# Chunk attention and a bilinear feed-forward: float32 loads by 256-token unit on one hardware queue, casts on chip, eight units transposed by TensorE in a hand-written order, one attention slot per unit

## The chip, the cores and the metric

The kernel runs on one core of one Trainium2 chip. The metric is device time in microseconds (us) of one execution, the median of several. A profile comes from one execution; its span, first to last instruction, is about 2 us shorter than the time. Words used below: TensorE multiplies matrices (PE in the profile; PEld is its weight load), VectorE is DVE, ScalarE is ACT, GpSimd is POOL, and SP is the engine that issues the hardware DMA queue. PSUM is the memory that TensorE writes its results to; to evict is to copy them out of it.

## The reference, cut to what matters

```python
# q, k, v: (8, 8, 576, 64) float32; chunks of 64 tokens
scores = scale * q_c @ k_c.T           # per batch, head and chunk
attn = softmax(scores)
x = (attn @ v_c) as (4608 tokens, 512) # heads side by side
out = ((x @ w_a) * (x @ w_b)) @ w_out  # 512 -> 1536 -> 512
```

The kernel works on blocks of 512 tokens, nine in all. A block has two units of 256 tokens for the attention. The feed-forward part of a block is 12 column steps (8 matmuls each, two products and their multiplication) and 4 output steps (12 matmuls each). That makes 144 matmuls of 128x512 per block, 1296 in the program.

## The kernel before

Everything is loaded as float32 and cast to bf16 by the DMA itself, which is issued by GpSimd (the software queue). Units 0 to 3 are transposed by TensorE and later ones by a DMA transpose. TensorE's instructions are kept in the program's order:

```python
DMA_TRANSPOSE_FROM = 2                       # blocks 2 and up
...
nc.gpsimd.dma_start(out=dst[:, g0 + g],      # bf16 <- float32, 256-byte rows
    in_=src[bt, :, s0 + 128 * g:s0 + 128 * g + 128, :].rearrange("h p d -> p h d"))
...
if K >= DMA_TRANSPOSE_FROM:
    by_dma()
    return [scores, sums, values]            # three separate steps
return [by_pe, scores, sums, values]
...
for g in range(NG):                          # load order: block 0,
    load_rows(0, 128 * g, 128 * g + 128)
for i in range(3):
    load_ab_weights(512 * i, 512 * i + 512)  # all of w_a and w_b,
load_block(1)                                # block 1, then w_out, block 2
...
att = start_attention(K + 1) if K + 1 < NBLK else []   # while block K is fed forward
...
for i, s in enumerate(att):                  # TensorE order: from step 1 of the block on
    at.setdefault(1 + i * (n - 2) // len(att), []).append(s)
```

The softmax here doesn't subtract the row's maximum and nothing guards it: scores larger than these inputs give would overflow.

## Time and profile before

| | before |
|---|---|
| time, median of the first 3 runs | 354.98 us (354.16 to 356.6) |
| span of the profiled run | 352.6 us |
| first feed-forward matmul | 24.46 us |
| second unit pair needed by TensorE, and there | 31, 38.4 us |
| first DMA transpose needed, and there | 66, 70.9 us |
| period of a block later on | 33.9 us |

From the page of the kernel before: span, busy times, the span in 40 equal slices (each digit is the busy share in tenths; PEclk is the granted TensorE clock), and the chain of work that ended last. The clock record begins only at 30.0 us, so the PEclk digits before that say nothing: the first four feed-forward matmuls, at 24.46 in the timeline below, take 1.87 us, where later eight take 1.73.

```profile
span 352.6 us, 6180 instructions
...
PE 319.6 (91%) x2584; PEld 145.2 (41%) x2584; DVE 125.2 (36%) x167; ACT 118.3 (34%) x163; POOL 107.3 (30%) x134
...
PE   0545799499999999999999999999999999999994
...
PEclk9998599989999999999999999999999999999999
...
PE 85%; DMA 8%; POOL 5%; issue 0%; SPq 0%; DVE 0%; POOLq 0%
```

The first ten slices, 88 us, are where TensorE is not full. After them only its own work counts.

The stretch table of the kernel before: stretch, its length, busy time of each engine, granted clock, DMA share (the time of all packets over that of 16 engines; packets overlap, so it can be above 1), and GB/s.

```profile
10.00:12.00 2.00, 0.68 (x35) 0.43 (x33) 1.23 (x1) 0.00 (x0) 2.00 (x3) 1.00 2.29 146
18.00:20.00 2.00, 0.64 (x32) 0.55 (x33) 0.53 (x1) 0.72 (x1) 0.78 (x2) 1.00 1.23 207
90.00:120.00 30.00, 30.00 (x234) 13.31 (x232) 11.95 (x16) 12.08 (x18) 16.10 (x21) 1.00 1.88 168
```

GB/s counts written bytes. The cast halves them, so 146 and 207 are about 290 and 410 GB/s read.

The timeline of the kernel before, TensorE only (start, length, instruction, in brackets the idle time before it and what ended it):

```profile
24.46 1.87 PE L224 MATMUL mm<-xT,wb_sb 128*128 128x512 bf16 x4 [3.04 <-DVE xT L195]
34.15 0.58 PE L129 MATMUL att<-identity,q_raw 128*128 128x128 bf16 x4 [3.35 <-DMA q_raw<-in_q_dram]
38.38 0.61 PE L129 MATMUL att<-identity,k_raw 128*128 128x128 bf16 x4 [1.56 <-DMA k_raw<-in_k_dram]
70.88 0.60 PE L153 MATMUL att<-qkt 64*64 64x64 bf16 x32 [5.22 <-DMA qkt<-k_raw]
```

Feed-forward starts at 24.46. TensorE then waits for q and k of unit 2, and again at 66 to 71 for the transposed k of unit 4.

The same kernel's chain of waits in order of time (start, length, what), the loads that ended the first wait, and one step that comes once per block:

```profile
15.82 16.56 DMA wb_sb<-in_moe_w_b_dram
...
34.40 3.93 DMA k_raw<-in_k_dram
...
61.37 9.46 DMA qkt<-k_raw
...
97.34 0.38 PE att L187 x32
...
131.24 0.38 PE att L187 x32
```

The last weights land at 15.82 + 16.56 = 32.4 us and the k that TensorE needs at 38.3. One period is 131.24 - 97.34 = 33.9 us.

### The profile page before, as it was taken

How to read it: one execution, taken by the hardware profiler on the slowest of the kernel's cores; microseconds unless marked ns; L12 is line 12 of the kernel's file. 1: busy time of each engine (PE TensorE's matmuls, PEld its weight loads, DVE VectorE, ACT ScalarE, POOL GpSimd, SP SyncE). 2: the span in 40 equal slices, each digit the busy share in tenths (PEclk: the TensorE clock that was granted, in tenths of full speed). 3: DMA queues.
4: the chain of work that ended last, by engine and by line, in shares of the span. 5: the costliest groups of instructions: out<-in, count | busy, mean ns of one | idle time of the engine just before them, and what ended most of it. 6: DMA issues, size and time to landing. Idle time of an engine off the chain costs nothing.

```text
span 352.6 us, 6180 instructions
## 1 busy us (share of the span) xinstructions
PE 319.6 (91%) x2584; PEld 145.2 (41%) x2584; DVE 125.2 (36%) x167; ACT 118.3 (34%) x163; POOL 107.3 (30%) x134
## 2 busy tenths in 40 slices
PE   0545799499999999999999999999999999999994
PEld 0422344144444444444444444444444444444441
DVE  0321255214353434244333434343435343433331
ACT  1331146132525143434333434333442434311210
POOL 8924949396345865931200000000000000000000
PEclk9998599989999999999999999999999999999999
DMA  9999999999999999995933324320211111111213
GB/s 77 166 207 158 145 176 154 147 158 160 159 183 173 175 174 172 170 182 120 72 79 70 81 18 92 73 60 3 60 32 30 30 33 30 32 30 31 61 30 89
DMA packets 152603, 36.05 MB, mean 102 GB/s; under 512 B 143360, under 2 KB 147968, under 8 KB 152576
## 3 DMA queue, kind: packets, MB, share of 16 engines
q0 software_dynamic: 117248, 18.88, 73.2%
q1 hardware_dynamic: 35328, 16.79, 25.5%
q8 instruction: 20, 0.33, 0.4%
q14 instruction: 7, 0.06, 0.0%
HBM read 37.75 MB, written 9.44 MB: 134 GB/s over the span
## 4 chain that ended last, share of the span: by engine, by line
PE 85%; DMA 8%; POOL 5%; issue 0%; SPq 0%; DVE 0%; POOLq 0%
PE mm L224 52%; PE mm L241 27%; DMA wb_sb<-in_moe_w_b_dram 5%; DMA qkt<-k_raw 3%; PE att L153 2%; PE att L187 2%; PE att L168 2%; POOL q_raw L101 2%; DMA k_raw<-in_k_dram 1%; POOL v_raw L101 1%; POOL k_raw L101 1%; POOL wa_sb L66 1%; PE att L129 0%; POOL wb_sb L66 0%; SPq L138 0%
## 5 line engine op out<-in xcount | busy, mean ns | idle before, releaser
L224 PE MATMUL mm<-xT,wb_sb 128*128 128x512 bf16 x432 | 114.2, 388 | 3.0 <-DVE xT L195 3.0
L234 DVE TENSOR_TENSOR ab_sb<-mm,b_sb 128x512 bf16<-128x512 f32 x108 | 74.7, 692 | 116.9 <-PE mm L224 116.9
L233 ACT CAST b_sb<-mm 128x512 bf16<-128x512 f32 x108 | 63.3, 586 | 157.5 <-PE mm L224 157.5
L224 PE MATMUL mm<-xT,wa_sb 128*128 128x512 bf16 x432 | 112.9, 384 | 0.0
L241 PE MATMUL mm<-wo_sb,ab_sb 128*128 128x512 bf16 x432 | 100.2, 383 | 0.0
L224 PEld LDWEIGHTS <-wa_sb 128*128 128x128 bf16 x432 | 42.8, 99 | 52.7 <-issue 3.0
L241 PEld LDWEIGHTS <-ab_sb 128*128 128x128 bf16 x432 | 41.5, 99 | 50.7 <-issue 3.5
L224 PEld LDWEIGHTS <-wb_sb 128*128 128x128 bf16 x432 | 40.0, 99 | 50.0 <-issue 7.0
L249 DVE COPY o_sb<-mm 128x512 f32<-128x512 f32 x36 | 24.9, 692 | 79.4 <-PE mm L241 77.1
L160 ACT ACTIVATE E<-att 128x1024 bf16<-128x1024 f32 x18 | 18.4, 1024 | 48.8 <-PE att L153 48.8
L101 POOL DMA_DIRECT2D v_raw<-in_v_dram x32 | 28.7, 910 | 16.4 <-PE att L187 12.4
L101 POOL DMA_DIRECT2D k_raw<-in_k_dram x32 | 28.5, 902 | 15.8 <-DMA q_raw<-in_q_dram 7.5
L101 POOL DMA_DIRECT2D q_raw<-in_q_dram x32 | 28.8, 915 | 9.5 <-DMA q_raw<-in_q_dram 2.8
L195 DVE TENSOR_TENSOR xT<-att,rs 128x1024 bf16<-128x1024 f32 x18 | 21.9, 1217 | 9.3 <-ACT rs L177 9.3
L176 ACT ACTIVATE ln<-att 128x1024 f32<-128x1024 f32 x18 | 18.4, 1024 | 11.6 <-PE att L168 11.6
L177 ACT ACTIVATE rs<-ln 128x1024 f32<-128x1024 f32 x18 | 19.0, 1058 | 0.3
L153 PE MATMUL att<-qkt 64*64 64x64 bf16 x576 | 8.8, 205 | 8.2 <-DMA qkt<-k_raw 5.2
L129 PE MATMUL att<-identity,q_raw 128*128 128x128 bf16 x32 | 4.0, 284 | 13.2 <-DMA q_raw<-in_q_dram 12.5
L153 PEld LDWEIGHTS <-qkt 64*64 64x64 bf16 x576 | 6.7, 117 | 16.0 <-issue 6.3
L134 DVE COPY qkt<-att 128x2048 bf16<-128x2048 bf16 x4 | 4.9, 1222 | 16.9 <-PE att L129 16.8
L168 PE MATMUL att<-E,ones 64*64 64x512 bf16 x72 | 7.8, 424 | 2.3 <-ACT E L160 2.3
L187 PEld LDWEIGHTS <-v_raw 64*64 64x64 bf16 x576 | 6.8, 114 | 7.2 <-issue 6.7
(19 smaller groups left out, 46.6 us busy)
## 6 DMA issues: line engine op xcount, KB each, us to landing
out_dram<-o_sb SPq DMA_DIRECT2D x72, 128.0 KB, 2.4
q_raw<-in_q_dram POOLq DMA_DIRECT2D x32, 128.0 KB, 8.9
k_raw<-in_k_dram POOLq DMA_DIRECT2D x32, 128.0 KB, 7.8
v_raw<-in_v_dram POOLq DMA_DIRECT2D x32, 128.0 KB, 8.3
wa_sb<-in_moe_w_a_dram POOLq DMA_DIRECT2D x3, 512.0 KB, 11.1
wb_sb<-in_moe_w_b_dram POOLq DMA_DIRECT2D x3, 512.0 KB, 12.8
wo_sb<-in_moe_w_out_dram POOLq DMA_DIRECT2D x2, 768.0 KB, 10.1
q_raw<-in_q_dram POOLq DMA_DIRECT2D x8, 64.0 KB, 10.9
```

The costliest lines, as they stand in the source:

```text
L101: nc.gpsimd.dma_start(out=dst[:, g0 + g], in_=src[bt, :, s0 + 128 * g:s0 + 128 * g + 128, :].rearrange("h p d -> p h d"),)
L153: nc.tensor.matmul(sc[cl * 64:cl * 64 + 64, j, m, gg, :], qkt[j * 64:j * 64 + 64, 1, gg, m, cl * 64:cl * 64 + 64], qkt[j * 64:j * 64 + 64, ...
L160: nc.scalar.activation(out=E, in_=sc, func=AF.Exp, scale=scale)
L168: nc.tensor.matmul(sm[j * 64:j * 64 + 64, cl, :], ones[cl * 64:cl * 64 + 64, :], E[cl * 64:cl * 64 + 64, j].rearrange("p m g s -> p (m g s)"),
L176: nc.scalar.activation(out=ln.rearrange("p c m n -> p c (m n)"), in_=sm, func=AF.Ln)
L177: nc.scalar.activation(out=rs, in_=ln, func=AF.Exp, scale=-1.0)
L195: nc.vector.tensor_tensor(out=dst, in0=av.rearrange("p c m g s -> p c m (g s)"), in1=rs, op=mybir.AluOpType.mult,)
L224: nc.tensor.matmul(t[:, sp * w:sp * w + w], wt[:, kt, cols], xT[:, kt, sp * w:sp * w + w], start=(kt == 0), stop=(kt == NKT - 1),)
L233: nc.scalar.copy(out=b_sb, in_=ps[0])
L234: nc.vector.tensor_tensor(out=ab_tiles[K][:, ft, :], in0=ps[1], in1=b_sb, op=mybir.AluOpType.mult)
L241: nc.tensor.matmul(o_ps, ab_tiles[K][:, ft, tg * 128:tg * 128 + 128], wo_sb[:, ft, :], start=(ft == 0), stop=(ft == NFT - 1),)
L249: nc.vector.tensor_copy(out=o_sb, in_=o_ps)
```

## The change

The intent: all loads go as float32 through one hardware queue in an explicit order, so that what is needed first comes first, and the casts move to VectorE (units 0 to 7 and the weights) and GpSimd (later units). Eight units are transposed by TensorE instead of four. The order of TensorE's work in blocks 0 and 1 is written out by hand: block 0 is fed forward with only unit 2's transposes in between, and block 1 is done in two halves of 256 tokens. Sums of the last unit, scores of the next and values of the last follow each other in one slot, and all of PSUM is one pool of eight banks. Cut to its core:

```diff
-DMA_TRANSPOSE_FROM = 2
+PE_UNITS = 8
...
-            nc.gpsimd.dma_start(
-                out=dst[:, :, c0:c1],
+            staged[n, i] = wst_pool.tile([128, NKT, WCOL], FP32, name="wst")
+            nc.sync.dma_start(
+                out=staged[n, i],
...
+            eng = nc.vector if U < PE_UNITS else nc.gpsimd
+            eng.tensor_copy(out=raw[n, U], in_=staged.pop((n, U)))
...
+    def slot(s=None, f=None):
+        if f is not None:
+            sums(f)
+        if s is not None:
+            scores(s)
+        if f is not None:
+            values(f)
...
-    with tc.manual_schedule(engines={mybir.EngineType.PE}):
+    with tc.manual_schedule(engines={mybir.EngineType.PE, mybir.EngineType.SP}):
+        load_qk(0)
+        load_qk(1)
+        load_v(0)
+        load_v(1)
+        for i in range(3):
+            load_ab(i)
...
+        for i in range(NWP):                  # block 0
...
+            if i + 3 < NWP:
+                load_ab(i + 3)
+            if i == 3:
+                load(2)
+                load(3)
+            ab_step(0, 2 * i)
+            if i == 5:
...
+                cast(2, "qk")
...
+                transpose_pe(2)
+            ab_step(0, 2 * i + 1)
+        slot(2)
+        cast(2, "v")
+        load_v(5)
+        slot(None, 2)
...
+        seq = [lambda ft=ft: ab_step(1, ft, 0, 256) for ft in range(NFT)]
+        seq += [lambda ft=ft: ab_step(1, ft, 256, 512) for ft in range(NFT)]
...
+                seq.insert(12, lambda: slot(2 * K + 4, 2 * K + 3))    # blocks 2 to 7
...
+                seq.insert(4, lambda: slot(2 * K + 3, 2 * K + 2))
```

## The prediction

> **What bounds the kernel now.** The chain of waits is 85% TensorE, 8% DMA. The stretch table shows TensorE full (30.0 of 30 us) from 90 us on, and the chain repeats a block every 33.9 us: 144 feed-forward matmuls at 0.216 us (31.1 us) plus two attention units at 1.4 us, each in three pieces. The sum closes: last matmul 347.8 = 35.3 (effective start: feed-forward begins at 24.5 but only 2 of 12 steps run before TensorE waits, 31 to 38.4, for unit 2's q and k, queued behind all first weights) + 280 (1296 x 0.216) + 1.8 (half-clock matmuls at 38.8 to 42.4) + 19.6 (14 units x 1.4) + 3.7 (units 2, 3) + 7.5 (5.2 us waiting at 66 to 71 for the first DMA transpose, then a cold clock). The tail is 4.8. So about 43 us of 353 are start and stalls. Meanwhile written bytes run at 205 GB/s (twice that read) for weights but about 150 (300 read) for 256-byte q, k, v rows.
>
> **What the change does.**
> - Order and queue: q, k of units 0, 1 first, in 512-byte runs, then v, then weights in small pieces. The same read bytes at 300 to 400 GB/s put k of unit 1 at about 9 us, the first weights at 16, all a/b weights at 29, unit 2 at 34, before TensorE wants it. The start is then bound by the attention chain, not loads. VectorE keeps order: it casts unit 1 before it evicts unit 0's transposes. Estimate: scores 0 at 11.4, scores 1 at 15, xT at 22.5; feed-forward starts at 22.6 and should not stop: -12.7.
> - Casts on chip: 42 on VectorE, 30 on GpSimd. The Trainium skill ("VectorE: DVE Perf Modes", the perf-mode tier table) gives an fp32 SBUF copy twice the base rate, so I estimate 0.65 us for 1024 columns. In block 1 VectorE is then about 35 of 40 us busy: +3 of local stalls.
> - Transposes by TensorE for 8 units, not 4: 16 took 0.89 us, +4.5, but no wait for a DMA transpose and its cold clock: -7.5.
> - New wait: after block 0, unit 2 runs alone (scores, exp, sums, ln, exp, multiply) with nothing to fill TensorE: +4.4, perhaps +1 cold clock. Half-width matmuls in block 1: +0.5. Start clock +0.7.
> - One slot per unit: the three pieces cost 0.48, 0.44, 0.48 us, about 0.1 each for re-entering; the skill ("TensorEngine Tiling (Array Packing)", Key Properties) says changing tiling mode drains TensorE. I estimate 1.1 instead of 1.4: -4.8 over 16 units, less 1.5 for bunched evictions (8 shared PSUM banks).
>
> Sum: about -9.4, giving 345.6; the schedule looks hand-fitted, so some of my stalls may be absent: **343 us**, 8 in 10 within **334 to 352**. Faster by over 2%: **0.73**; within 2%: **0.23**; slower: **0.04**.
>
> **What would show it.** First feed-forward matmul at 21 to 24 us, no wait over 2 us in block 0; about 5 us idle once near 45 to 50 us; no wait for DMA transposes; period 33.2 to 33.6 us from block 3 on; casts 0.6 to 0.7 us; loads of q, k, v spread to the end.
>
> **What would make it wrong.** Hardware-queue loads of 256-byte runs well under 250 GB/s, or in-order waits of that queue (stores, transposes and loads share it) starving a unit: +5 to +15. Casts at 1.1 us: VectorE binds block 1, +5 to +8. Bunched evictions stalling each slot: the period stays 33.9. Against that, an earlier start or a cheaper slot: to 334.

## The result

The changed kernel takes 340.49 us (median of 4 runs, 340.02 to 340.7), the kernel before 354.57 in the same rounds. The ratio is 0.959, with a 95% interval of 0.9551 to 0.963. Here and below, a ratio is the mean time of one kernel's runs over that of the other's of the same rounds, so it is not quite the ratio of the medians. Executions over 1.5% slower than the fastest of the same kernel are left out of the means.

The page of the changed kernel, the lines that answer to those before:

```profile
span 338.6 us, 6687 instructions
...
PE 313.0 (92%) x2709; PEld 160.6 (47%) x2744; DVE 158.9 (47%) x251; ACT 129.8 (38%) x227; POOL 31.9 (9%) x36
...
PE   2459959999999999999999999999999999999994
...
PEclk9999996999999999999999999999999999999999
...
PE 90%; ACT 3%; DMA 2%; DVE 1%; issue 1%; SPq 1%
```

TensorE is now full from the fourth slice on, except for one dip in the sixth, and no DMA of importance is left in the chain.

Its timeline, TensorE only, the two waits of 1 us or more from the first feed-forward matmul to the end, and between them the place where TensorE starts on unit 2, without a wait:

```profile
22.31 0.59 PE L280 MATMUL ps<-xT,wb_307 128*128 128x512 bf16 x1 [3.10 <-DVE xT L241]
...
42.84 0.61 PE L164 MATMUL ps<-identity,q_raw 128*128 128x128 bf16 x8
...
51.14 1.01 PE L280 MATMUL ps<-xT,wb_307 128*128 128x256 bf16 x4 [3.30 <-DVE xT L241]
```

Its chain of waits, first where only unit 2 runs, then half-width matmuls at full clock, then one slot and the next one at the same place a block later:

```profile
45.63 0.44 PE ps L194 x32
46.07 1.07 ACT E L202 x2
47.19 0.43 PE ps L209 x3
47.62 1.07 ACT ln L219 x2
48.71 1.06 ACT rs L222
49.84 0.57 issue
50.41 0.69 DVE xT L241
51.14 5.23 PE ps L280 x24
...
62.76 7.09 PE ps L280 x64
...
134.99 0.34 PE ps L209 x4
135.33 0.28 PE ps L194 x32
135.61 0.32 PE ps L232 x32
...
168.16 0.34 PE ps L209 x4
```

Feed-forward starts 2.15 us earlier and runs through block 0. Then 5.5 us pass from the scores of unit 2 to the first matmul of block 1. The clock record has half clock from 49.4 to 56.2, and the 24 half-width matmuls after the wait take 5.23 us. Later 64 of them take 7.09, so 24 would take 2.66: the clock costs 2.6 us. The period is 168.16 - 134.99 = 33.17 us.

Two numbers speak against the reading that the loads which TensorE stood waiting for now come earlier. The trace's landings have the last piece of w_a and w_b at 32.4 us in both kernels, and k of unit 2 at 37.7 us (before: 38.3). What differs is that TensorE doesn't ask for unit 2 until 42.8 us. Only the very first loads are earlier: k of unit 1 lands at 9.25 us (before: 15.0), which goes with the earlier start. So the experiments below ask which part of the change did it.

### The profile page after: what moved, and what is told of

Its sections match the earlier page's. It is cut to its first block, busy times and chain, and to the rows that moved or that the text cites. A ratio compares the mean times of both kernels' runs of the same rounds, so it can differ in the third digit from the quotient of the medians.

```text
span 338.6 us, 6687 instructions
## 1 busy us (share of the span) xinstructions
PE 313.0 (92%) x2709; PEld 160.6 (47%) x2744; DVE 158.9 (47%) x251; ACT 129.8 (38%) x227; POOL 31.9 (9%) x36
## 4 chain that ended last, share of the span: by engine, by line
PE 90%; ACT 3%; DMA 2%; DVE 1%; issue 1%; SPq 1%
PE ps L280 56%; PE ps L296 27%; PE ps L164 2%; DMA k_in<-in_k_dram 2%; PE ps L209 2%; PE ps L194 2%; PE ps L232 1%; ACT rs L222 1%; ACT ln L219 1%; ACT qkt L172 1%; SPq L128 1%; DVE xT L241 1%; ACT E L202 0%; DVE qkt L172 0%; DVE k_raw L152 0%
## 5 line engine op out<-in xcount | busy, mean ns | idle before, releaser
L288 ACT CAST b_sb<-ps 128x512 bf16<-128x512 f32 (+1 forms) x120 | 64.3, 546 | 145.3 <-PE ps L280 121.6
L289 DVE TENSOR_TENSOR ab_sb<-ps,b_sb 128x512 bf16<-128x512 f32 (+1 forms) x120 | 75.6, 637 | 82.9 <-PE ps L280 80.2
L296 PEld LDWEIGHTS <-ab_sb 128*128 128x128 bf16 x432 | 42.2, 98 | 49.9
L304 DVE COPY o_sb<-ps 128x512 f32<-128x512 f32 x36 | 24.9, 691 | 54.8 <-PE ps L296 54.8
L241 DVE TENSOR_TENSOR xT<-ps,rs 128x512 bf16<-128x512 f32 x36 | 23.2, 686 | 30.1 <-ACT rs L222 30.1
L219 ACT ACTIVATE ln<-ps 128x512 f32<-128x512 f32 x36 | 19.7, 602 | 24.5 <-PE ps L209 24.5
L280 PE MATMUL ps<-xT,wb_307 128*128 128x512 bf16 (+1 forms) x79 | 20.3, 381 | 6.6 <-DVE xT L241 6.4
L152 POOL CAST q_raw<-q_in 128x1024 bf16<-128x1024 f32 x10 | 10.4, 1040 | 145.3 <-DMA q_in<-in_q_dram 130.2
L296 PE MATMUL ps<-wo_964,ab_sb 128*128 128x512 bf16 x72 | 21.4, 379 | 0.3
L296 PE MATMUL ps<-wo_1007,ab_sb 128*128 128x512 bf16 x72 | 21.4, 379 | 0.1
L296 PE MATMUL ps<-wo_1022,ab_sb 128*128 128x512 bf16 x72 | 21.4, 379 | 0.0
L296 PE MATMUL ps<-wo_992,ab_sb 128*128 128x512 bf16 x71 | 21.2, 379 | 0.0
L202 ACT ACTIVATE E<-ps 128x512 bf16<-128x512 f32 x36 | 19.3, 586 | 3.5 <-PE ps L194 3.5
L280 PE MATMUL ps<-xT,wa_309 128*128 128x512 bf16 (+1 forms) x80 | 20.5, 383 | 0.0
L296 PE MATMUL ps<-wo_949,ab_sb 128*128 128x512 bf16 x66 | 20.1, 379 | 0.3
L296 PE MATMUL ps<-wo_934,ab_sb 128*128 128x512 bf16 x67 | 20.3, 379 | 0.0
L280 PE MATMUL ps<-xT,wb_358 128*128 128x512 bf16 (+1 forms) x74 | 19.0, 365 | 0.3
L280 PE MATMUL ps<-xT,wa_360 128*128 128x512 bf16 (+1 forms) x80 | 19.2, 365 | 0.0
L280 PE MATMUL ps<-xT,wa_429 128*128 128x512 bf16 (+1 forms) x80 | 18.8, 358 | 0.4
L280 PE MATMUL ps<-xT,wb_461 128*128 128x512 bf16 (+1 forms) x74 | 18.6, 357 | 0.4
L280 PE MATMUL ps<-xT,wb_393 128*128 128x512 bf16 (+1 forms) x80 | 18.8, 358 | 0.0
```

The costliest lines, as they stand in the source:

```text
L152: eng.tensor_copy(out=raw[n, U], in_=staged.pop((n, U)))
L202: nc.scalar.activation(out=E_of[U][:, j], in_=sc[j], func=AF.Exp, scale=scale)
L219: nc.scalar.activation(out=ln[:, cl].rearrange("p m n -> p (m n)"), in_=sm[cl], func=AF.Ln)
L241: nc.vector.tensor_tensor(out=x_tiles[K][:, :, c0:c0 + 128], in0=av[cl].rearrange("p m g s -> p m (g s)"), in1=rs[:, cl], op=MULT,)
L280: nc.tensor.matmul(ps[n], w_ab[n, i][:, kt, o:o + 128], xT[:, kt, c0:c1], start=(kt == 0), stop=(kt == NKT - 1),)
L288: nc.scalar.copy(out=b_sb[:, :c1 - c0], in_=ps["wb"])
```

## The experiments

Theory A: the gain comes from TensorE's order in the first blocks, from the units that TensorE transposes itself, and from the slots. Theory B: it comes from the loads, that is from the hardware queue and the order of loading. The names b... are edits of the kernel before, a... of the changed one.

### b1_order: only TensorE's order in block 0

```diff
+            if K == 0:
+                for j, i in zip((0, 1, 4, 2, 5, 3, 6, 7), (7, 8, 8, 9, 9, 10, 10, 11)):
+                    at.setdefault(i, []).append(att[j])
+                att = []
```

> The kernel before with TensorE's order of block 0 changed alone: unit 2 and 3's attention steps come after feed-forward step 7 instead of after step 1. Loads, queue, casts untouched. Theory A (the wait from 31 to 38.4 us is TensorE's fixed order asking for unit 2 too early, not the loads being late): the wait goes, feed-forward still starts at 24.5 us, at most 1.5 us of waiting is left before block 1, time 354.6 - 7 to - 9, so 345.5 to 348. Rival B (the gain of the change comes from load order and the hardware queue): nothing much changes, within 2 us of 354.6.

Measured: 354.37 us, ratio 0.9985 (0.9949 to 1.0021). The same, as B said, but not for B's reason. The timeline of b1_order, the two waits of over 2 us that follow its first feed-forward matmul:

```profile
53.32 1.02 PE L224 MATMUL mm<-xT,wb_sb 128*128 128x512 bf16 x3 [2.19 <-DVE xT L195]
...
72.68 0.64 PE L153 MATMUL att<-qkt 64*64 64x64 bf16 x32 [15.75 <-DMA qkt<-k_raw]
```

The waiting between 31 and 38 us is gone, exactly as A said, and the wait for the DMA transpose of unit 4 grew from 5.2 to 15.75 us. It ends near the same time as before (72.7, was 70.9). TensorE reached the second wait earlier and stood there longer.

### b2_pe_transposes: only eight units transposed by TensorE

```diff
-DMA_TRANSPOSE_FROM = 2
+DMA_TRANSPOSE_FROM = 4
```

> The kernel before with 8 units transposed by TensorE instead of 4, nothing else. Theory: the 5.2 us wait for the first DMA transpose at 66 to 71 us and the half clock after it (together 7.5) go, four units more at 0.9 us on TensorE (+3.6): 350.7, range 349 to 352. Rival (the DMA transposes only wait because loads are late, so the wait moves to the loads of units 4 and 5): the wait stays at about 4 us near 66 us and the time is 354 to 358.

Measured: 350.96 us, ratio 0.9896 (0.9857 to 0.9934), the expected 350.7. The wait near 66 us is gone; the one from 31 to 38 us is still there. Its start in the timeline of b2_pe_transposes:

```profile
34.86 0.59 PE L129 MATMUL att<-identity,q_raw 128*128 128x128 bf16 x4 [4.43 <-DMA q_raw<-in_q_dram]
```

### b3_both: both edits

> The kernel before with both earlier edits: block 0's TensorE order changed and 8 units transposed by TensorE. In the order-alone run the 7.4 us wait at 31 to 38 us only moved: the wait for the DMA transpose of unit 4 grew from 5.2 to 15.7 us and ended at the same 72 us. Theory (two waits in series on one stream of loads and transposes, so each edit alone leaves the other in charge): together they give much more than the sum of 0.4 and 3.8: unit 4's k lands near 62 us instead of its transpose at 72.6, a wait of 3 to 6 us is left in block 1, time 345 to 349. Rival (the two edits just add): 350 to 351.

Measured: 344.71 us, ratio 0.9729 (0.9704 to 0.9753). Alone the edits gave 0.4 us, which is within the noise, and 3.8 us (354.74 the median of before in their rounds, 354.69 here), together 10.0. The longest wait on a DMA after the start of the timeline of b3_both is this:

```profile
59.06 0.40 PE L129 MATMUL att<-identity,k_raw 128*128 128x128 bf16 x4 [1.29 <-DMA k_raw<-in_k_dram]
```

The theory had expected 3 to 6 us of waiting in block 1, and the time came out just under its range.

The two waits were thus in series, and while the second stood, the first was worth nothing. The kernel still uses the old software queue, the old load order and the old three-piece attention. Ten of the fourteen microseconds come without any of them.

### a1_split: the slot undone in blocks 2 to 7

```diff
-                seq.insert(12, lambda: slot(2 * K + 4, 2 * K + 3))
...
-                seq.insert(4, lambda: slot(2 * K + 3, 2 * K + 2))
+                for at, s, f in ((12, 2 * K + 4, 2 * K + 3), (4, 2 * K + 3, 2 * K + 2)):
+                    seq.insert(at + 2, lambda f=f: values(f))
+                    seq.insert(at + 1, lambda s=s: slot(s))
+                    seq.insert(at, lambda f=f: sums(f))
```

> The changed kernel with the slot undone in blocks 2 to 7: sums, scores and values separated by one feed-forward or output step each. Theory (each re-entry from the small tiles to the full array costs about 0.1 to 0.2 us, three instead of one per unit): period 33.17 goes to 33.8 to 33.9, time 340.5 + 4 (12 slots x 0.35), 343.5 to 345.5. Rival (the shorter period comes from the shared PSUM banks and the changed evictions): period stays at 33.2, time within 1 us of 340.5.

Measured: 344.88 us, ratio to the kernel before 0.9712 (0.9679 to 0.9744); the changed kernel has 340.49. Its chain of waits, one place a block apart:

```profile
135.96 0.41 PE ps L209 x4
136.37 1.83 PE ps L280 x8
138.20 0.38 PE ps L194 x32
...
169.86 0.41 PE ps L209 x4
```

The period is back at 33.90 us, and the 4.4 us are 12 slots at 0.37 us. The sums, scores and values take 0.41 + 0.38 + 0.38 = 1.17 us apart, and 0.34 + 0.28 + 0.32 = 0.94 in one slot. The rest of the 0.37 is in the matmuls after each piece: the 8 after the sums take 1.83 us here, and 8 undisturbed ones 1.73, and this 0.1 us is paid three times instead of once. The shared PSUM pool stayed, so it is not what shortened the period by itself.

### a4_software_queue: the changed kernel's loads back on the software queue

```diff
-            staged[n, i] = wst_pool.tile([128, NKT, WCOL], FP32, name="wst")
-            nc.sync.dma_start(
+            staged[n, i] = wpool.tile([128, NKT, WCOL], BF16, name=f"{n}{i}")
+            nc.gpsimd.dma_start(
...
-            eng = nc.vector if U < PE_UNITS else nc.gpsimd
-            eng.tensor_copy(out=raw[n, U], in_=staged.pop((n, U)))
+            raw[n, U] = staged.pop((n, U))
```

The same for q, k, v and w_out; the units that TensorE transposes take two DMAs per piece instead of one, with 256-byte rows. The input tiles get more buffers (6 or 8, not 3), and the cast tiles are gone.

> The changed kernel with its loads back on the GpSimd software queue that casts in the DMA; no staging, no casts on VectorE or GpSimd; order of loads and of TensorE as in the change. Theory A (TensorE's order and the slots make the gain, the hardware queue and the casts on chip don't): first feed-forward matmul at 20 to 23 us (VectorE no longer casts unit 1 before it evicts unit 0), time 337 to 342. Rival B (the hardware queue makes the gain): q and k of unit 1 come later, first feed-forward matmul at 24 us or later, waits for loads in block 1, time 344 to 350.

Measured: three fast runs at 340.56 to 341.51 us, ratio 0.9604 (0.9573 to 0.9635), where the changed kernel has 0.959. The profiled run was a slow one (586.92 us): its clock record stands at 0.16 from 285.5 us to the end, and is like the others before that. There the first feed-forward matmul is at 21.72 us, and TensorE waits for unit 2 alone, as in the changed kernel:

```profile
21.72 0.59 PE L272 MATMUL ps<-xT,wb 128*128 128x512 bf16 x1 [3.10 <-DVE xT L233]
...
50.66 1.01 PE L272 MATMUL ps<-xT,wb 128*128 128x256 bf16 x4 [3.30 <-DVE xT L233]
```

So the hardware queue, the 512-byte runs and the casts on chip make none of the gain within 1 us. a4 keeps the new order of loads, and no run put the old order back alone: what that order is worth, in the earlier start above all, is not measured. The Trainium skill ("DMA: Bandwidth & Descriptors", Issuing engines are not separate DMA queues) says that DMAs of all issuing engines end up on the same 16 DMA engines and interleave. The 340.6 to 341.5 here fit that, but they are no test of it, because few waits for loads are left to shorten.

### a2_early_unit2: unit 2 inside block 0

```diff
         for i in range(3):
             load_ab(i)
+        load(2)
...
             ab_step(0, 2 * i)
+            if i == 3:
+                cast(2, "qk")
+                transpose_pe(2)
+            if i == 4:
+                slot(2)
+                cast(2, "v")
             if i == 5:
...
+                slot(None, 2)
             ab_step(0, 2 * i + 1)
-        slot(2)
...
-        slot(None, 2)
```

> The changed kernel with unit 2 loaded right after the third weight piece (the queue stood waiting there for a staging buffer) and its attention run inside block 0 (transposes after step 6, scores after step 8, sums and values after step 10) instead of alone after it. Theory (the 5.5 us at 45.6 to 51.1 in which only unit 2 runs, and the half clock of 6.8 us it brings, are pure loss): 340.5 - 4.4 - 2.6, so 333 to 335.5. Rival (weights now come later and block 0 stalls for them, or the clock drops anyway later): 337 to 341.

Measured: 339.43 us (338.29 to 340.68), ratio 0.957 (0.9535 to 0.9605). The rival was nearer: only 1.1 us came of the expected 5 to 7.5, and with runs spread over 2.4 us and an interval that holds the changed kernel's 0.959, even that is not clear of the noise. Two new waits, in its timeline:

```profile
37.17 1.39 PE L280 MATMUL ps<-xT,wb 128*128 128x512 bf16 x3 [2.06 <-DVE wb L85]
...
52.99 0.61 PE L280 MATMUL ps<-xT,wb 128*128 128x256 bf16 x4 [1.48 <-DVE xT L241]
```

The first is a wait for the cast of a weight piece, and half clock follows it (37.3 to 40.7 us in the clock record). Whether the weights came late or VectorE did is settled by a6 below.

### a3_pool_cast1: unit 1 cast by GpSimd

```diff
-            eng = nc.vector if U < PE_UNITS else nc.gpsimd
+            eng = nc.vector if U < PE_UNITS and (U != 1 or n == "v") else nc.gpsimd
```

> The changed kernel with q and k of unit 1 cast by GpSimd (idle then) instead of VectorE. Theory (VectorE, in order, holds unit 0's evictions behind the cast of unit 1's k, which lands at 9.25 us): scores of unit 0 start at 9.4 instead of 11.3, first feed-forward matmul at 20 to 21 instead of 22.3, time 338 to 339.5. Rival (the start is bound by ScalarE's chain or by the weights' cast): first feed-forward matmul still at 22, time 340 to 341.

Measured: 338.81 us (338.35 to 339.93), ratio 0.9556 (0.9533 to 0.958). All four runs lie below the changed kernel's fastest (340.02). Scores of unit 0 start at 9.39 us (11.26 in the changed kernel) and the first feed-forward matmul at 20.44, in the timeline of a3_pool_cast1:

```profile
9.39 0.64 PE L194 MATMUL ps<-qkt 64*64 64x64 bf16 x32 [1.41 <-ACT qkt L172]
...
20.44 0.59 PE L280 MATMUL ps<-xT,wb 128*128 128x512 bf16 x1 [3.10 <-DVE xT L241]
```

The theory holds. VectorE's fixed order had put two evictions behind a cast that waited for a load.

### a5_both and a6_pool_weights: towards a better kernel

a5_both is a2 and a3 together.

> The two edits of the changed kernel together: unit 2 early and unit 1 cast by GpSimd. Theory: they add, 331.5 to 334. Rival (an earlier start only makes block 0 wait for weights or for unit 2): the same as unit 2 early alone within 0.5.

Measured: 337.59 us, ratio 0.9513 (0.9479 to 0.9547). They add within the spread of the runs (1.1 and 1.7 alone, 2.9 together), but 331.5 to 334 was not reached, because a2 hadn't been worth 7. The two waits are those of a2, 2 us earlier. In a5's trace, the weight piece that TensorE waits for lands at 29.9 us and is cast at 34.48, after three casts of unit 2. a6_pool_weights takes those casts from VectorE and brings unit 2's sums and values one step earlier:

```diff
-            nc.vector.tensor_copy(out=w_ab[n, i], in_=staged.pop((n, i)))
+            eng = nc.vector if i < 3 else nc.gpsimd
+            eng.tensor_copy(out=w_ab[n, i], in_=staged.pop((n, i)))
...
-        nc.vector.tensor_copy(out=t, in_=staged.pop(("wo", i)))
+        nc.gpsimd.tensor_copy(out=t, in_=staged.pop(("wo", i)))
...
             if i == 4:
                 slot(2)
                 cast(2, "v")
+                ab_step(0, 9)
+                slot(None, 2)
+                continue
```

> The two edits together (unit 2 early, unit 1 cast by GpSimd) left two waits: 2.06 us for a weight cast that VectorE did after unit 2's casts and evictions (with 3.4 us of half clock after it) and 1.48 us for unit 2's multiply. Here the weight pieces from the fourth on and all output weights are cast by GpSimd, and unit 2's sums and values come one step earlier. Theory (VectorE's fixed order, not the loads, held those casts): both waits and the half clock go, 337.6 - 2.1 - 1.7 - 1.5, so 331.5 to 333.5. Rival (the loads of the weights come too late once unit 2 goes before them): a wait of 1 us or more for weights stays near 35 us, time 335 to 338.

Measured: 333.14 us (333.03 to 334.39), ratio 0.9406 (0.9384 to 0.9428). This beats both kernels. The timeline of a6_pool_weights has only these waits on VectorE left after the first matmuls:

```profile
33.37 1.04 PE L281 MATMUL ps<-xT,wa 128*128 128x512 bf16 x4 [0.15 <-DVE ab_sb L290]
45.78 0.61 PE L281 MATMUL ps<-xT,wb 128*128 128x256 bf16 x4 [0.62 <-DVE xT L242]
```

The clock stays full from 23.7 us to the last matmul. So the load was in time, and VectorE's order was what held the weight piece: the theory given for a2 was right about the loss, and wrong that moving unit 2 was enough.

### a7_software_early: the software queue again, with unit 2 early

It is a4 with the block 0 order of a6 (no casts, so none to move).

> The software-queue version (casts in the DMA, no casts on any engine) with unit 2 early and its sums and values inside block 0. Theory (the hardware queue and the casts on chip are not what makes the gain, and without casts VectorE can't hold anything up): no wait over 1 us after feed-forward starts, time 331 to 335, as good as the hardware queue with the casts moved to GpSimd. Rival (the hardware queue brings the loads earlier, which matters once the other waits are gone): weights or unit 2 late, waits of 2 us or more in block 0, time 336 to 341.

Measured: 335.03 us (334.27 to 335.17), ratio 0.9444 (0.9429 to 0.9458). No wait of over 1 us is left after feed-forward starts at 21.60 us. It is 1.9 us slower than a6, and its feed-forward starts 1.15 us later (20.45 there). Of the other 0.7 us, about 0.4 lies outside the span (a7's times are 2.2 us longer than their spans, a6's 1.8); the rest I did not trace. So the hardware queue, with its 512-byte runs, is worth about 1 us of start, once a free engine does the casts.

## Why the prediction was right, point by point

The prediction was 343 us in 334 to 352, and 340.49 was measured. Its sum closes on the measured trace as well: 334.2 (last matmul) = 22.3 (start) + 279.9 (1296 x 0.216) + 5.3 (six units transposed by TensorE at 0.89) + 5.5 (unit 2 alone) + 2.6 (half clock after it) + 15.5 (15 slots, each (33.17 - 31.1) / 2 = 1.03) + 3.1, which is the remainder. By estimates from the trace, 1.6 of it is the cold start (feed-forward at half rate from 22.3 to 25.5), 0.5 the half-width matmuls of block 1 (192 at 0.111 us instead of 96 at 0.216), and most of the rest small waits.

- **"Feed-forward starts at 22.6 and should not stop."** Right: 22.31, and no stop in block 0.
- **"Order and queue: -12.7."** The size was about right and the name was wrong. The prediction gave the credit to loads that come before TensorE wants them. The loads it named were to land at 29 (all a/b weights) and 34 us (unit 2), and they came no earlier than before (32.4 us in both kernels, 37.7 against 38.3 for k of unit 2). Only k of unit 1 came as predicted (9.25), and so did the start. a4 loses at most 1 us without the queue. What counted was that TensorE asks for unit 2 later.
- **"No wait for a DMA transpose and its cold clock: -7.5", added to the -12.7.** b1, b2 and b3 show that these don't add as separate terms: the order alone is worth 0.4 us, the transposes alone 3.8, both 10.0 (net of the transposes' cost). The sum came out right only because the change did both; that was luck.
- **"Transposes by TensorE +4.5."** Slightly too large. The 16 transposes of a unit take 0.89 us in the changed kernel too, and TensorE does four more units than before, so they cost 3.6 us.
- **"Unit 2 runs alone: +4.4, perhaps +1 cold clock."** The wait was right: 5.5 us, of which 1.1 was counted as the unit's slot. The clock was mis-sized: 2.6 us. The Trainium skill ("TensorE: Matmul & The Clock Gate", Part 1) puts the return to half clock at an idle window of about 3.4 us. Here it came sooner. The half clock began at 49.4 us, 1.5 us into the wait of 3.30 us, when TensorE had still been busy for 1.1 of the last 3.4 us, and it lasted 6.8 us. In a2 a wait of 2.06 us was enough; in b1 one of 2.19 us, ended at 53.3, brought no half clock.
- **"One slot per unit 1.1 instead of 1.4: -4.8, less 1.5 for bunched evictions."** The slot costs 1.03, and a1 measures 4.4 us for 12 of them. Bunched evictions cost nothing that the period shows: 33.17 us, just below the predicted 33.2 to 33.6.
- **"Casts 0.65 us, local stalls +3."** The casts took 0.67 to 0.69 us on VectorE, close to the estimate made from the page's rate; only one, at 89.4 us, took 1.16, while GpSimd was casting too. The stalls were too large: VectorE was busy for 29.7 of the 40 us from 51 to 91 (35 predicted), and there TensorE waited 0.4 us in two waits, for evictions by ScalarE.
- **"Loads of q, k, v spread to the end."** Wrong: the last of them is issued at 196.1 us of 338.6.

The terms of the prediction come to 345.6; the step from there to 343 was a guess without a term behind it, and luck in that sense. Against the terms, by estimates from the traces, the local stalls were 2.6 us smaller, the slots 2.2 better (15 at 0.37 against 4.8 - 1.5), the transposes 0.9 cheaper, and the 1.8 us of half-clock matmuls at 38.8 to 42.4 went too, which the prediction has in its sum for the kernel before but not in the change; the clock after unit 2 cost 1.6 more. Together that is 5.9, where 345.6 - 340.5 = 5.1 was seen. The effects of b3 (10.0) and of the slots (4.4) come to 14.4, and the whole gain is 14.1. That they agree is no proof that they are independent, because the changed kernel also starts 2 us earlier and loses 8 us with unit 2 alone, which b3 doesn't.

## What to carry to other kernels

When an engine with a fixed order waits for a load, look first at how early its order asks for it, and then at the next wait behind it: removing the first of two waits in series may only lengthen the second. An edit that measures nothing alone may be worth most of the gain with its partner, so try the pair before you drop it. Casts and evictions on one in-order engine wait for each other's inputs; give those that depend on loads to an engine that is idle.

## What the Trainium skill lacked or had wrong

- "DMA: Bandwidth & Descriptors" says that all issuing engines share the 16 DMA engines. It has no figure for what that does to a DMA transpose. From issue to landing it took 8.1 us (median) beside software-queue loads in the kernel before, and 2.9 in the changed kernel. The least was 2.7 in both. With the loads of the changed kernel back on the software queue it took 8.3 (a7), on the hardware queue with nearly the same order of work 2.9 (a6).

In the traces, before and then changed, issue to landing of the transposes' target:

```profile
DMA to landing us min/median/max: 2.7/8.1/10.4
```

```profile
DMA to landing us min/median/max: 2.7/2.9/5.0
```

- "TensorEngine Tiling (Array Packing)", Key Properties, says that a change of tiling mode drains TensorE, and gives no cost. Here three visits to the small tiles instead of one cost 0.37 us per unit (a1), so by that estimate about 0.18 us for each further visit.
- "TensorE: Matmul & The Clock Gate", Part 1, has half clock after an idle window of about 3.4 us. Here waits of 3.30 us (1.5 us into it) and 2.06 us (a2) brought it. The page warns of a clock seen stuck at a quarter for 50 us and more. It does not have what one run of a4 showed: a clock of 0.16 for the last 301 us, and 586.9 us instead of 341, in one execution of four. Its cause is open.
- "GPSIMD Engine Reference", 4.1 Engine selection, calls one-input work on GpSimd roughly line-rate and gives no time for a cast. Here a float32 to bf16 cast of 128x1024 took 1.04 us on GpSimd and 0.69 us on VectorE, and moving casts there paid off (a3, a6).
